# Head outputs turned by one transposing DMA per chunk, running sums accumulated in PSUM, and GpSimd's early work queued by the planner

## The chip, the cores and the metric

The kernel runs on one core of a Trainium2 chip. The metric is the device time of one execution in microseconds (us). The kernel before takes 731.63 us in the median of 3 runs (731.5 to 731.91).

## The reference

One input x of 2048 tokens by 512 features goes through two branches, and a gate mixes them per token.

```python
g = _sigmoid((x * gate_w).sum(-1, keepdims=True))
# A: 32 query heads of 16 dims, one shared K and V head
q = (x @ wq) as 32 heads;  k = x @ wk;  v = x @ wv
p = softmax(q k^T * 16 ** -0.5)        # 2048 x 2048 for each head
a = concat_heads(p @ v) @ wo           # 512 x 512
# B: gated MLP with a token-mixing matrix
z = gelu(x @ w_in)                     # 2048 x 1376
z1, z2 = z[..., :688], layernorm(z[..., 688:])
b = (z1 * (w_sp @ z2 + b_sp)) @ w_out  # w_sp is 2048 x 2048
return g * a + (1 - g) * b
```

All inputs and the output are bfloat16. Most of the work is the 32 x 2048 x 2048 exponentials of the softmax.

## The kernel before

**Units and blocks.** Attention is cut into 32 units: unit `u` is query chunk `c = u // 8` (512 queries) and four of the 32 heads. A unit has 64 blocks: 16 key tiles `kt` of 128 keys, times the four heads `g`. A block is one TensorE matmul of 32 rows (`s_mm`, tile `QA,KA`), one exponential of 128 x 512 scores, and one matmul with V that adds to the unit's output in a PSUM bank (`o_mm`). Two heads share 32 partitions of the queries `QA`. Even units read `KA[:, 0]`, where K fills the first 16 rows of each 32; odd units read `KA[:, 1]`, a copy shifted by 16 rows, which SyncE's queue (SP) makes by a DMA per chunk of 512 keys (`ld_K1`, L299). The input chunks arrive in the order `XO = (0, 3, 2, 1)`, so chunk 1, key tiles 4 to 7, is the last of the four.

**Two engines make the exponentials.** ScalarE (ACT) does most blocks, two or three at a time, by `Exp` from PSUM into the ring `P` (`exp_op`, L783). VectorE (DVE) does up to `NMAX` = 8 key tiles of a unit by a polynomial: `d_A` (L795) evacuates a block from PSUM into `UW[:, 0]`, `d_u` (L800) squares it, and `d_w` (L806) squares it again into `UW[:, 1]`; some of the `d_w` pieces go to GpSimd (POOL). Four blocks of one key tile are a batch. Both squares are multiplied with V on TensorE, and the constant and linear terms of the polynomial come from two small tables over V: `SVB` (sums of V, `g_SV`) and `KTV` (sums of K times V, `g_KTV`), each a running sum over the 8 key tiles. `KF` and `SF` are the fp32 sums, kept in the tail of tile `z1`, which the profile prints as `z`.

**After a unit.** DVE turns the unit's output out of PSUM (`t1_op`, L820). For two units together DVE takes a reciprocal, and POOL multiplies it by the gate (`rr`) and scales the output into `Tn` (`norm_ops`, L827). DVE turns `Tn` back by 32 x 32 blocks into `OT` (`t2_op`, L851). When the four pairs of a chunk are in `OT` and branch B's product `u` is there, `g_out` (L722) accumulates six matmul groups of branch B and four of `wo` with `OT` in one PSUM bank, and the result goes out. Chunk 3 is finished at the end by `g_part`, `g_fin` and `g_out` so that little is left after unit 31.

**The order is written by a planner.** `build_kernel` simulates PE, ACT and DVE with fixed costs (`C_MM`, `C_EV`, `A_OV`, ...) and emits each instruction when its turn comes, so each engine's program is a fixed list, run in order, with semaphore waits from the data dependencies. POOL's work is in two kinds: what is emitted on the spot, with its time only added up by `pool_t` (L404), and what waits in the queue `pl_q` until `pool_try` (L1604) finds that DVE will be reading PSUM for a while. SP has no clock in the planner. Each DMA of SP is put into SP's list when the planner reaches the call, and SP runs that list in order. A chained load (`sp_dma`, L276) waits on SP for the chained load before it to have landed. For the shifted copy of K the planner reckons a due time of its own:

```python
spc["free"] = max(spc["free"], t) + 650.0
T[("K1", c)] = spc["free"] + 2300.0
```

Before, the loads of `wo`, `wout` and the first quarter of `wT` (turned by DMA, four pieces) are issued by `g_K`'s `done` for the last chunk, right after that chunk's `ld_K1`. A second, general program for inputs on which the polynomial isn't safe follows behind a flag and is not executed here.

Of the kernel before, what the change touches and what calls it, by code (L numbers as in the profile page):

```python
# [19 lines left out]
NKT = 16  # L20
# [5 lines left out]
NQ = 3  # L26
# [32 lines left out]
PR = dict(HALF=100.0, IDR=10, IDN=4, WRES=16, D_HG=2500.0, D_FL=False, WIN=1000.0, WIH=560.0, BACK=32, PRESS=5, FLEX=3500.0, RMIN=32, WBL=0.5, W_MIN=0.9, HOLD=0.0, RLEND=0)  # L59
# [109 lines left out]
def build_kernel(nc, x_d, wq_d, wk_d, wv_d, wo_d, win_d, wsp_d, bsp_d, wout_d, gw_d, out_d):  # L169
    es = ExitStack()  # L170
    with es:
# [37 lines left out]
        OT = sb("OT", [128, 2, 4, 512], B16)  # L209
# [32 lines left out]
        wq_raw = UW[:, 1, ND - 1, :].bitcast(B16).rearrange("p (a n) -> p a n", a=4)  # L242
        z1 = z1f[:, 0:5 * S].rearrange("p (f t) -> p f t", t=S)
# [67 lines left out]
        def ld_wo(q):  # L311
            out = []
            for g in range(4):
                for jj in range(2):
                    out.append(q.dma_start(wo[32 * g + 16 * jj:32 * g + 16 * jj + 16, :, :],
                                           wo_d.rearrange("(jp r) n -> r jp n", r=128)[64 * jj + 16 * g:64 * jj + 16 * g + 16, :, :]))
            return out
# [38 lines left out]
        def mm(dst, lhsT, rhs, start, stop, r, w, tp=None, chan=None, tag=""):  # L356
            def fn(t):
                if tp is None:
                    return t.matmul(dst, lhsT, rhs, start=start, stop=stop)
                return t.matmul(dst, lhsT, rhs, start=start, stop=stop, tile_position=tp)  # L360
            return op("pe", fn, r=r, w=w, chan=chan, tag=tag)

# [60 lines left out]
        def g_K(c, lo=0, hi=512, b=BM):  # L423
# [8 lines left out]
            def done(t):  # L432
# [17 lines left out]
        def g_k2(c):  # L450
# [5 lines left out]
            def rdy():  # L456
                if not started:
                    if c and ("k2", c - 1) not in T:
                        return None
                    ksq()  # L460
                    started.append(pool_t(1150.0) + L_X)
                return started[0]
# [33 lines left out]
        def g_V(c, b=BM):  # L496
# [37 lines left out]
        def g_SV():  # L534
            n0 = NKT - NMAX

            def piece():
                fm(BM, 32 * NMAX, 0, ones[:], V1[:, n0:NKT, :].rearrange("p k w -> p (k w)"), True, True, ["ones", ("V", 2), ("V", 3)], "SV")
# [5 lines left out]
            def done(t):  # L544
                for i in range(NMAX - 2, -1, -1):
                    op("pool", lambda g, i=i: g.tensor_tensor(SF[:, i, :], SF[:, i, :], SF[:, i + 1, :], ALU.add), r=["SF"], w=["SF"], tag="SF")
                op("pool", lambda g: g.tensor_copy(SVB[:, 0:NMAX, :], SF), r=["SF"], w=["SVB"], tag="SVB")
                op("pool", lambda g: g.tensor_tensor(SVB[64:128, 0:NMAX, :], SF[64:128, :, :], SVB[64:128, 0:NMAX, :], ALU.subtract),
                   r=["SF", "SVB", ("z1", 5)], w=["SVB"], tag="SVB")
                T["SVB"] = pool_t(7 * 400.0 + 1200.0, t) + L_X  # L550
            return Group([(150.0, piece)], [(350.0, ev)], lambda: when(("V", 2), ("V", 3)), done, tag="SV")

        def g_KTV():
            n0 = NKT - NMAX

            def piece(k, e):
                def f():
                    for q in range(4):
                        o = 512 * BM + 64 * k + 32 * e
                        mm(ps[32 * q:32 * q + 32, o:o + 32], KN[:, k, e, :], V1[:, n0 + k, :], True, True,  # L560
# [3 lines left out]
            def ev():  # L564
                op("dve", lambda v: v.tensor_scalar(KF, bank(BM, 64 * NMAX).rearrange("p (k e w) -> p k e w", e=2, w=32), Q_C1, None, ALU.mult),
                   r=[bkey(BM), ("z1", 5)], w=["KF"], tag="KTVev")

            def done(t):
                for i in range(NMAX - 2, -1, -1):
# [5 lines left out]
            return Group([(26.0, piece(k, e)) for k in range(NMAX) for e in range(2)], [(C_EV, ev)], lambda: when(("V", 2), ("V", 3)), done, tag="KTV")  # L575

        def gate():
            op("act", lambda a: a.activation(E[:], gs[:], ACT.Exp), r=[("gs", k) for k in range(4)], w=["E"], tag="E")
            t = clk["now"] + 350.0
            for g in range(4):  # L580
                for k in range(4):
                    op("pool", lambda p, g=g, k=k: p.tensor_copy(RT[32 * g:32 * g + 32, :, :].rearrange("p c b -> p (c b)").rearrange("p (n k) -> p n k", k=4)[:, :, k],
                                                                E[32 * k:32 * k + 32, :]), r=["E"], w=["RT"], tag="RT")
            T["RT"] = pool_t(16 * 280.0, t) + L_X
# [18 lines left out]
        def gelu_ops():  # L603
            out = []
            for k in range(4):
# [32 lines left out]
                out.append((2400.0, f, []))  # L638
            for ft in range((NZ - ZD) // 4):
# [3 lines left out]
                out.append((1810.0, f, [("z1", ft, tc) for tc in range(4)]))  # L643
# [44 lines left out]
        def g_part(t2):  # L688
# [6 lines left out]
            def pw(jp):  # L695
                return lambda: fm(BM, 512, 0, OT[:, 1, jp, 128 * i:128 * i + 128], wo[:, jp, :], False, jp == 2, [("OT", 1, jp), "wo"], "wo")
# [4 lines left out]
            return Group([(C_MM, py(ft)) for ft in range(6)] + [(C_MM, pw(jp)) for jp in range(3)], [(C_EV + 50.0, ev)],  # L701
                         lambda: when(*([("u", ft, 3) for ft in range(6)] + [("OT", 3, jp) for jp in range(3)])), setT(("pt", i)), tag="part")

        def g_fin(t2, b, ready, eng):
# [3 lines left out]
            def piece():  # L708
                fm(b, 512, 0, OT[:, 1, 3, 128 * i:128 * i + 128], wo[:, 3, :], True, True, [okey, "wo"], "wo")
# [12 lines left out]
        def g_out(t2, b=BM, ready=None, on_act=False, eng="sp"):  # L722
# [67 lines left out]
        def o_mm(u, g, lhsT, rhs, r, last):  # L790
# [1125 lines left out]
```

## Time and profile before

| | |
|---|---|
| median of 3 runs | 731.63 us |
| the profiled execution, its own time | 731.97 us |
| its span in the trace | 730.0 us |
| busy: PE, DVE, ACT, POOL | 709.3, 711.0, 710.7, 471.9 us |
| ACT exponentials | 738 instructions, 1492 blocks |
| DVE batches | 139 |

The span is what the trace covers from the first instruction to the last; the execution's own time is 1.97 us longer. TensorE's busy time holds matmuls with zeros that the planner puts into idle stretches (tile `CT,zer`). In a timeline row the first number is the start in us and the second the time from the first instruction of the row to the end of its last; "x4" is the number of instructions that were merged. `[0.43 <-PE ps L360]` is idle time of the engine before the row, and what ended it.

### The profile page before, as it was taken

What the parts mean: (1) busy time and instruction counts of PE and PEld (TensorE: products, weight loads), DVE (VectorE), ACT (ScalarE), POOL (GpSimd) and SP (SyncE); (2) the same over time, 40 slices, a digit from 0 to 9 for tenths busy, and PEclk for the clock granted to TensorE, in tenths of its full rate; (3) what the DMA queues carried; (4) which work ended last, traced back from release to release, by engine and by line L of the source; (5) the groups of instructions that cost most, each with busy time, mean ns of one, the idle gap of its engine ahead of it and who ended that gap; (6) DMA issues with size and microseconds to landing.
All of it is one profiled execution on the core that took longest, in us unless ns stands there. A gap on an engine that the chain in (4) does not pass through costs nothing.

```text
span 730.0 us, 21704 instructions
## 1 busy us (share of the span) xinstructions
PE 709.3 (97%) x9004; PEld 207.4 (28%) x9004; DVE 711.0 (97%) x1028; ACT 710.7 (97%) x757; POOL 471.9 (65%) x439
## 2 busy tenths in 40 slices
PE   7999999999999999999999999999999999999996
PEld 3323333323322223222222232222222222222322
DVE  5999999999999999999999999999999999999996
ACT  5999999999999999999999999999999999999995
POOL 6743666670267777667576777777777766777662
PEclk9999999999999999999999999999999999999999
DMA  8342000000000002200000042000002400000000
GB/s 160 121 101 59 2 1 2 2 3 2 2 2 1 3 2 63 70 17 2 1 2 2 2 88 52 9 2 2 2 2 57 76 17 1 2 2 1 2 3 32
DMA packets 49119, 17.72 MB, mean 24 GB/s; under 512 B 44244, under 2 KB 48504, under 8 KB 49016
## 3 DMA queue, kind: packets, MB, share of 16 engines
q1 hardware_dynamic: 46760, 16.00, 9.4%
q8 instruction: 71, 1.16, 0.6%
q10 hardware_dynamic: 2256, 0.30, 0.3%
q14 instruction: 32, 0.26, 0.1%
HBM read 3.25 MB, written 2.10 MB: 7 GB/s over the span
## 4 chain that ended last, share of the span: by engine, by line
PE 59%; ACT 21%; DVE 11%; issue 7%; DMA 1%; ACTq 0%
PE ps L360 59%; ACT P L785 21%; DVE UW L797 4%; DVE bst L613 2%; DVE UW L810 2%; DVE UW L804 2%; DVE z L627 1%; DMA wvg<-in_gate_w_dram 1%; DVE T L822 0%; ACT z L607 0%; DVE mv L617 0%; DVE QA L486 0%; DVE Tn L845 0%; ACT L607 0%; DVE z L599 0%
## 5 line engine op out<-in xcount | busy, mean ns | idle before, releaser
L785 ACT ACTIVATE P<-ps 128x1024 bf16<-128x1024 f32 (+1 forms) x738 | 685.4, 1179 | 8.6 <-PE ps L360 8.3
L810 POOL TENSOR_TENSOR UW<-UW 128x512 f16<-128x512 f16 (+1 forms) x282 | 369.6, 1311 | 163.3 <-DVE UW L810 63.6
L797 DVE TENSOR_SCALAR UW<-ps 128x512 f16<-128x512 f32 (+1 forms) x414 | 347.7, 861 | 1.7 <-PE ps L360 1.1
L360 PE MATMUL ps<-QA,KA 32*128 32x512 bf16 x2048 | 311.7, 384 | 10.1 <-ACT P L785 5.3
L360 PE MATMUL ps<-P,V 128*32 128x512 bf16 x1492 | 207.2, 385 | 0.2 <-DVE KN L514 0.2
L804 DVE TENSOR_TENSOR UW<-UW 128x2048 f16<-128x2048 f16 (+1 forms) x166 | 174.4, 1052 | 1.1
L360 PEld LDWEIGHTS ps<-QA,KA 32*128 32x128 bf16 x2048 | 83.8, 91 | 310.8 <-ACT P L785 159.3
L360 PE MATMUL ps<-UW,VW 128*32 128x512 f16 x556 | 117.5, 384 | 0.2 <-DVE UW L810 0.2
L360 PE MATMUL ps<-wT,z 128*32 128x512 bf16 (+1 forms) x1536 | 115.9, 366 | 0.0
L810 DVE TENSOR_TENSOR UW<-UW 128x1024 f16<-128x1024 f16 (+4 forms) x173 | 112.3, 660 | 0.2
L360 PE MATMUL ps<-UW,V 128*32 128x512 f16 x556 | 83.9, 384 | 1.2 <-DVE T L822 0.7
L360 PEld LDWEIGHTS ps<-P,V 128*32 128x32 bf16 x1492 | 47.7, 94 | 52.4 <-issue 48.5
L490 POOL TENSOR_TENSOR QSQ<-QA 128x512 bf16<-128x512 bf16 x16 | 26.4, 1648 | 23.2 <-DVE UW L797 10.5
L360 PEld LDWEIGHTS ps<-wT,z 128*32 128x32 bf16 x1536 | 28.8, 94 | 43.2 <-issue 41.8
L360 PEld LDWEIGHTS ps<-UW,VW 128*32 128x32 bf16 x556 | 27.8, 94 | 15.9 <-issue 11.9
L360 PE MATMUL ps<-wout,z 128*32 128x512 bf16 x384 | 31.8, 384 | 0.0
L360 PE MATMUL ps<-win,xT 128*32 128x344 bf16 x512 | 31.0, 312 | 0.7 <-DVE QA L486 0.7
L845 POOL TENSOR_TENSOR Tn<-T,rc 128x512 bf16<-128x512 f32 x15 | 22.9, 1526 | 8.0 <-DVE UW L797 4.0
L360 PEld LDWEIGHTS ps<-UW,V 128*32 128x32 bf16 x556 | 19.6, 94 | 18.4 <-issue 11.7
L822 DVE STREAM_TRANSPOSE T<-ps 128x512 f32<-128x512 f32 (+1 forms) x33 | 22.7, 691 | 2.1 <-PE ps L360 1.9
L360 PE MATMUL ps<-CT,SVB 128*32 128x512 bf16 x128 | 22.9, 384 | 0.0
L360 PE MATMUL ps<-xT,win 128*32 128x512 bf16 (+1 forms) x384 | 22.5, 363 | 0.2 <-ACT P L785 0.2
(113 smaller groups left out, 373.2 us busy)
## 6 DMA issues: line engine op xcount, KB each, us to landing
out_dram<-outsb SPq DMA_DIRECT2D x15, 128.0 KB, 1.7
win<-in_B_w_in_dram SPq DMA_DIRECT2D x1, 1376.0 KB, 6.3
wout<-in_B_w_out_dram SPq DMA_DIRECT2D x1, 640.0 KB, 5.3
wo<-in_A_wo_dram SPq DMA_DIRECT2D x8, 64.0 KB, 2.3
KA<-KA SPq DMA_DIRECT2D x4, 112.0 KB, 2.3
UW<-in_A_wq_dram SPq DMA_DIRECT2D x1, 384.0 KB, 4.1
wT<-in_B_w_sp_dram SPq DMA_TRANSPOSE x16, 4.3
UW<-in_A_wq_dram ACTq DMA_DIRECT2D x1, 128.0 KB, 3.6
```

Source lines behind the costliest of these rows:

```text
L360: return t.matmul(dst, lhsT, rhs, start=start, stop=stop, tile_position=tp)
L490: dq(pl_q, 1050.0, lambda: op("pool", lambda v: v.tensor_tensor(QSQ[:, q % 2, :], QA[:, q % NQ, :], QA[:, q % NQ, :], ALU.mult), r=[("Q", ...
L613: dq(dve_q, 410.0, lambda st=st, h=h: op("dve", lambda v: v.bn_stats(bst[:, st, h, :], z2[:, FH * st + 344 * h:FH * st + 344 * h + 344]), ...
L627: op("pool" if st in ZP else "dve", lambda v: v.tensor_scalar(z2[:, FH * st:FH * st + FH], z2[:, FH * st:FH * st + FH], mv[:, st, 0:1], rs ...
L785: op("act", lambda a: a.activation(P[:, 512 * p0:512 * (p0 + n)], ps[:, 512 * b0:512 * (b0 + n)], ACT.Exp), r=[bkey(b0 + i_) for i_ in ran ...
L797: op("dve", lambda v: v.tensor_scalar(UW[:, 0, s, 512 * i:512 * (i + n)], bank(b, 512 * n), Q_A, Q_AS, ALU.mult, ALU.add), r=[bkey(b + j) ...
L804: op("dve", lambda v: v.tensor_tensor(src, src, src, ALU.mult), r=k, w=k, tag="dTT")
L810: op(eng, lambda v: v.tensor_tensor(UW[:, 1, s, 256 * a:256 * b], src, src, ALU.mult), r=[("U", s, h) for h in range(a // 2, (b + 1) // 2) ...
L822: return lambda: pgx.op("dve", lambda v: v.transpose(T1[:, jj, c0:c1], bank(BO, c1 - c0, c0)), r=[bkey(BO)], w=[("T1", jj, c0)], tag="T1")
L845: pgx.op(eng, lambda v: v.tensor_tensor(tnv[:, pr, j0:j1, b0:b1, :], t1v[:, j0:j1, b0:b1, 0:16], rc[:, j0:j1, b0:b1].unsqueeze(3).broadcas ...
```

## The change

1. **`OT` by DMA.** For all but the last pair of chunk 3, POOL writes the scaled outputs of a chunk into one 128 x 2048 tile `TB[c]` (the output buffer `outsb` for chunk 0, parts of `win` for the others), and one DMA on SP turns the whole chunk into `OT` (`t2_dma`). 15 DVE transposes go. The last pair of chunk 3 keeps the DVE transpose, into `OT3`, with a copy of its rows of `wo` in `wo3`; its place in the chunk's tile is zeroed, so chunk 3 has five `wo` groups instead of four.
2. **Running sums in PSUM.** `g_SV` and `g_KTV` let TensorE add up the running sums: matmul number k writes k + 1 columns groups by a broadcast V. The 14 adds on POOL go. `KF` becomes bfloat16, and the four copies of `KF` into `KTV` go from POOL to SP: four DMAs of 32 x 16 pieces of 32 elements.
3. **POOL's early work in `pl_q`.** `KSQ`, `VW`, `SVB` and the gate's table `RT` are queued.
4. **Loads.** The loads of `wo`, `wout` and `wT` move from the last `g_K` to `g_KTV`'s `done`, behind the `KTV` DMAs.
5. **Costs.** `A_OV`, `FLEX` and the gelu costs are raised a little. The planner then writes another order: 140 batches instead of 139, and on ACT 738 exponentials over 1488 blocks (720 of two blocks, 15 of three, 3 of one; before 718, 18 and 2).

```diff
-        KF = tmp[:, 0:64 * NMAX].rearrange("p (k e w) -> p k e w", e=2, w=32)
+        KF = tmp[:, 0:32 * NMAX].bitcast(B16).rearrange("p (k e w) -> p k e w", e=2, w=32)
...
         def ld_wo(q):
+            return [q.dma_start(wo[16 * r:16 * r + 16, :, :], wo_d[64 * r:64 * r + 64, :].rearrange("(g d) n -> d g n", g=4)) for r in range(8)]
...
                 elif hi == 512 and c == XO[3]:
                     ld_K1(c, t)
                     ld_bsp(0)
-                    sp_dma(ld_wo, w=["wo"], n=128)
-                    ld_rest()
...
-                    ksq()
-                    started.append(pool_t(1150.0) + L_X)
+                    started.append(None)
+                    dq(pl_q, 1150.0, ksq, clk["now"], setT(("ksq", c)))
...
             def done(t):
-                for i in range(NMAX - 2, -1, -1):
-                    op("pool", lambda g, i=i: g.tensor_tensor(KF[:, i, :, :], KF[:, i, :, :], KF[:, i + 1, :, :], ALU.add), r=["KF"], w=["KF"], tag="KF")
                 for q in range(4):
-                    op("pool", lambda g, q=q: g.tensor_copy(KTV[32 * q:32 * q + 32, :, :, q, :], KF[32 * q:32 * q + 32, :, :, :]),
-                       r=["KF", ("z1", 5)], w=["KTV"], tag="KTV")
-                T["KTV"] = pool_t(7 * 430.0 + 4 * 720.0, t) + L_X
+                    op("sp", lambda d, q=q: d.dma_start(KTV[32 * q:32 * q + 32, :, :, q, :], KF[32 * q:32 * q + 32, :, :, :]),
+                       r=["KF", ("z1", 5)], w=[("KTV", q)], dma=16, after=[o_ktv], tag="KTV")
+                T["KTV"] = t + 6000.0
+                sp_dma(ld_wo, w=["wo"], n=128)
+                ld_rest()
...
+        def t2_dma(c, t):
+            assert c < 2 or ("o", 4 * c - 5) in T, c
+            op("sp", lambda q: q.dma_start_transpose(OT[:, c % 2, :, :], TB[c]), r=TBK[c], w=[("OT", c % 2)], dma=16, tag="T2")
+            T[("OT", c)] = t + C_T2
...
-                dq(pl_q, C_TN, tn, (lambda: when(("rr", u))), setT(("TnE", u // 2)))
-                dq(t2_q, 625.0, t2_op(pg, c, jp, 0, 512, [("Tn", pr, 0, 0), ("Tn", pr, 1, 0)]), (lambda: when(("TnE", u // 2), *([("o", 4 * c - 5)] if c > 1 else []))), setT(("OT", c, jp)))
+                def tne(t):
+                    T[("TnE", u // 2)] = t
+                    if jp == (2 if c == 3 else 3):
+                        t2_dma(c, t)
+                dq(pl_q, C_TN, tn, (lambda: when(("rr", u))), tne)
```

**SP, first part of its list.** The rows below are SyncE's queue in the first 65 us: the shifted copies of K (`KA<-KA`), the load of `win`, and what follows. `f_d4`, `f_d12` and so on are semaphores, one for each DMA (or group of eight); `f_dve` is DVE's. Before:

```order
L300 DMA KA<-KA 112x512 [waits f_pool,f_dve]
L300 DMA KA<-KA 112x512
L300 DMA KA<-KA 112x512 [waits f_dve]
L306 DMA win<-in_B_w_in_dram 128x4x1376 [waits f_d4]
L300 DMA KA<-KA 112x512 [waits f_dve]
L309 DMA bspz<-in_B_b_sp_dram 1x512 [waits f_d12,f_pool]
L315 DMA wo<-in_A_wo_dram 16x4x512 [waits f_d14]
L315 DMA wo<-in_A_wo_dram 16x4x512 x7
L328 DMA wout<-in_B_w_out_dram 128x5x512 [waits f_d15]
L330 DMA wout<-in_B_w_out_dram 48x512 [waits f_d16,f_pool]
L330 DMA wout<-in_B_w_out_dram 48x512 [waits f_d17]
L322 DMA_TRANSPOSE wT<-in_B_w_sp_dram 128x16x128 [waits f_d18]
```

Of the changed kernel, from the row behind `win` on:

```order
L591 DMA KTV<-z 32x16x32 [waits f_dve]
L591 DMA KTV<-z 32x16x32 x3
L318 DMA wo<-in_A_wo_dram 16x4x512 [waits f_d12]
L318 DMA wo<-in_A_wo_dram 16x4x512 x7
L345 DMA wout<-in_B_w_out_dram 128x5x512 [waits f_d17]
L347 DMA wout<-in_B_w_out_dram 48x512 [waits f_d18,f_pool]
L347 DMA wout<-in_B_w_out_dram 48x512 [waits f_d19]
L339 DMA_TRANSPOSE wT<-in_B_w_sp_dram 128x16x128 [waits f_d20]
L339 DMA_TRANSPOSE wT<-in_B_w_sp_dram 128x16x128 [waits f_d21]
L339 DMA_TRANSPOSE wT<-in_B_w_sp_dram 128x16x128 [waits f_d22]
L339 DMA_TRANSPOSE wT<-in_B_w_sp_dram 128x16x128 [waits f_d23]
L306 DMA KA<-KA 112x512 [waits f_dve]
```

The fourth copy of K, that of chunk 1, stood ahead of the loads of `wo`, `wout` and `wT`; it now stands behind all of them, and its semaphore is `f_d25` (before: `f_d13`).

**PE, where that copy is first read.** The rows are TensorE's list around the first matmul of unit 1 on key tiles 4 to 7 (`QA,KA` with a wait for the copy); `f_pes`, `f_pep` and `f_act` are semaphores of PE and ACT. Before:

```order
L360 MATMUL ps<-UW,VW 32x512 [waits f_dve]
L360 MATMUL ps<-P,V 32x512
L360 MATMUL ps<-UW,VW 32x512
L360 MATMUL ps<-QA,KA 128x512 [waits f_act,f_d13]
L360 MATMUL ps<-QA,KA 128x512
L360 MATMUL ps<-xT,wqd 32x512 [waits f_dve]
L360 MATMUL ps<-xT,wqd 32x512 x7
```

Of the changed kernel:

```order
L377 MATMUL ps<-xT,wqd 32x512 x4
L377 MATMUL ps<-P,V 32x512 x4
L377 MATMUL ps<-QA,KA 128x512 [waits f_act]
L377 MATMUL ps<-QA,KA 128x512 [waits f_d25]
L377 MATMUL ps<-P,V 32x512 x4
L377 MATMUL ps<-CT,zer 32x512 x4
L377 MATMUL ps<-UW,V 32x512 [waits f_dve]
```

The matmul stands at nearly the same place of the program: behind 97 matmuls of scores instead of 96, in ACT's 36th instead of its 37th exponential.

**DVE, where `KTV`'s sums leave PSUM.** The rows are DVE's list around the evacuations of `SF` and `KF` (both `z<-ps`). Before:

```order
L541 TENSOR_SCALAR z<-ps 128x256 [waits f_pe]
L797 TENSOR_SCALAR UW<-ps 128x512 [waits f_pes] x2
L804 TENSOR_TENSOR UW<-UW 128x2048 [waits f_dve]
L565 TENSOR_SCALAR z<-ps 128x512 [waits f_pe]
L797 TENSOR_SCALAR UW<-ps 128x1024 [waits f_pes]
```

Of the changed kernel:

```order
L565 TENSOR_SCALAR z<-ps 128x256 [waits f_pe]
L816 TENSOR_SCALAR UW<-ps 128x512 [waits f_pes]
L823 TENSOR_TENSOR UW<-UW 128x2048 [waits f_dve]
L816 TENSOR_SCALAR UW<-ps 128x1024 [waits f_pes]
L586 TENSOR_SCALAR z<-ps 128x512 [waits f_pe]
```

The evacuation of `KF` now follows one evacuation of 128 x 1024 that it was ahead of before.

More of the change, by code (lines that the diff above doesn't have):

```diff
@@ L256, in build_kernel @@
         op("dve", lambda v: v.memset(wk_rep[:], 0.0), w=["wk_rep"])
+        o_ktv = op("dve", lambda v: v.memset(KTV[:], 0.0), w=[("KTV", q) for q in range(4)])
         op("dve", lambda v: v.memset(V1[:], 0.0), w=[("V", c) for c in range(4)])
@@ L361, in mm, with wo_g @@
             return op("pe", fn, r=r, w=w, chan=chan, tag=tag)
+        def wo_g(b, c, i, g, start, stop, r):
+            for q in range(4):
+                mm(ps[32 * q:32 * q + 32, 512 * b:512 * b + 512], OT[:, c % 2, 4 * i + q, 32 * g:32 * g + 32], wo[:, g, :], start, stop, r, [bkey(b)],
+                   tp=(0, 32 * q), tag="wo")
         def fm(b, n, off, lhsT, rhs, start, stop, r, tag):
@@ L642, in f @@
                     T[("gelu", ft)] = clk["now"] + 2000.0
-                out.append((1810.0, f, [("z1", ft, tc) for tc in range(4)]))
+                out.append((1905.0, f, [("z1", ft, tc) for tc in range(4)]))
             return out
@@ L844, in d @@
             def d():
-                pgx.op(eng, lambda v: v.tensor_tensor(tnv[:, pr, j0:j1, b0:b1, :], t1v[:, j0:j1, b0:b1, 0:16],
+                dst = TB[c].rearrange("p (b z j w) -> p z j b w", z=4, j=2, w=16)[:, jp, :, :, :] if big else tnv[:, pr, j0:j1, b0:b1, :]
+                aft = list(pgx.ops["dve"][-2:-1]) if eng == "pool" else []
+                if big and c and jp == 0:
+                    assert dz["i"] >= NZ and dz["cur"] is None
+                    aft += pg.readers["win"][-1:]
@@ L1183, in f @@
                         def f(last, g=g, n=n, u=pu):
-                            o_mm(u, g, KTV[:, NMAX - n, u % 2, g, :], QA[:, (u // 2) % NQ, :], ["KTV", ("Q", (u // 2) % NQ)], last)
+                            o_mm(u, g, KTV[:, NMAX - n, u % 2, g, :], QA[:, (u // 2) % NQ, :], [("KTV", q) for q in range(4)] + [("Q", (u // 2) % NQ)], last)
                             if g == 3:
@@ L1357, in dz_act @@
                     T[("gelu", ft)] = t + L_X
-            return now + act_period(n)
+            return now + act_period(n) + 90.0
         def pe_work(now):
```

125 lines of the change are left out of this document (73 added, 52 removed).

## The prediction

> **What bounds the kernel now.** I read the page first, then ACT's groups by shape, the windows behind 45 us, ACT's waits, and last the rows of the two queues that the change reorders. The page:
>
> ```profile
> span 730.0 us, 21704 instructions
> PE 709.3 (97%) x9004; PEld 207.4 (28%) x9004; DVE 711.0 (97%) x1028; ACT 710.7 (97%) x757; POOL 471.9 (65%) x439
> ```
>
> Three engines look equally full, so the page alone doesn't say who leads. The windows (PE, PEld, DVE, ACT, POOL busy, then clock and DMA; the sum is over all five from 45 to 720 us) and ACT's waits do:
>
> ```profile
> 60.00:160.00 100.00, 97.89 (x1257) 30.82 (x1257) 99.24 (x138) 100.00 (x108) 62.57 (x51) 1.00 0.03 7
> ...
> 240.00:700.00 460.00, 457.64 (x5537) 125.55 (x5529) 457.14 (x626) 460.00 (x501) 326.26 (x272) 1.00 0.08 19
> ...
> sum 675.00, PE 665.50 PEld 191.08 DVE 670.17 ACT 672.94 POOL 440.00; mean PE 133.10 PEld 38.22 DVE 134.03 ACT 134.59 POOL 88.00
> ...
> ACT P L785 <- PE ps L360: 8.3, 10, 5.3
> ```
>
> From 60 to 160 and from 240 to 700 us ACT is busy for every microsecond; in the 675 us from 45 to 720 it idles 2.1. PE and DVE idle more there and are led by it: the end is ACT's number of exponentials, and whatever stops ACT. Of its 8.3 us of waits on PE, 5.3 are the start. ACT's work by shape:
>
> ```profile
> L785 ACT ACTIVATE P<-ps 128x1024 bf16<-128x1024 f32 x718 | 664.0, 1171 | 2.9 <-PE ps L360 2.7
> L785 ACT ACTIVATE P<-ps 128x1536 bf16<-128x1536 f32 x18 | 28.3, 1570 | 5.3 <-PE ps L360 5.3
> L785 ACT ACTIVATE P<-ps 128x512 bf16<-128x512 f32 x2 | 1.2, 594 | 0.3 <-PE ps L360 0.3
> ```
>
> An instruction overlaps the next, so its price is busy time over count: 664.0 / 718 = 0.925 us for two blocks, 28.3 / 18 = 1.57 for three, 0.6 for one.
>
> **The path that decides: the fourth copy of K.** Rows of the SP queue from 24 us on, the landing times (last number, us), and PE and ACT at the matmul that needs the copy of chunk 1:
>
> ```profile
> 28.22 0.51 SPq L300 DMA_DIRECT2D KA<-KA  x1
> ...
> 30.31 3.62 SPq L315 DMA_DIRECT2D wo<-in_A_wo_dram  x8
> 35.73 0.39 SPq L328 DMA_DIRECT2D wout<-in_B_w_out_dram  x1
> 41.05 2.07 SPq L330 DMA_DIRECT2D wout<-in_B_w_out_dram  x2
> 44.46 16.53 SPq L322 DMA_TRANSPOSE wT<-in_B_w_sp_dram  x4
> ...
> SPq L322 <- DMA wT<-in_B_w_sp_dram: 8.8, 3, 4.0
> ...
> KA<-KA SPq DMA_DIRECT2D x4, 112.0 KB, 2.3
> wT<-in_B_w_sp_dram SPq DMA_TRANSPOSE x16, 4.3
> ...
> 45.06 0.39 PE L360 MATMUL ps<-QA,KA 32*128 32x512 bf16 x2
> ...
> 45.38 0.61 PE L360 MATMUL ps<-xT,wqd 128*32 128x512 bf16 x8
> 45.52 1.02 ACT L785 ACTIVATE P<-ps 128x1024 bf16<-128x1024 f32 x1 [0.43 <-PE ps L360]
> ```
>
> In the trace the copy is issued at 28.22 and lands 2.3 later, 14 us before the matmul at 45.06 reads it. The loads behind it take SP from 30.31 to 60.99 (44.46 + 16.53), because each waits for the one before to land (8.8 us of waits among the `wT` pieces). In the changed kernel the copy stands behind these loads, and the matmul that needs it has kept its place. The planner's due time for the copy doesn't see SP's list. So:
>
> 1. `KF`'s evacuation. It frees the `KTV` DMAs, and with them the loads.
>
> ```profile
> 23.40 0.68 DVE L565 TENSOR_SCALAR z<-ps 128x512 f32<-128x512 f32 x1
> 24.00 1.21 DVE L797 TENSOR_SCALAR UW<-ps 128x1024 f16<-128x1024 f32 x1
> ```
>
> It ended at 24.1; now the 1.21 us evacuation stands ahead of it: 25.3. Bounds 24.1 (nothing moves) and 26.2 (`KTV`'s wider matmuls on PE push it too).
>
> 2. Four `KTV` DMAs. The trace has no DMA like them; a copy of K took 0.51 to issue, and `win` and `wk_sb`, both 512 pieces, show these rows:
>
> ```profile
> 18.24 0.59 SPq L306 DMA_DIRECT2D win<-in_B_w_in_dram  x1
> wk_sb<-in_A_wk_dram ACTq DMA_DIRECT2D x1, 16.0 KB, 2.1
> ...
> 36.21 0.38 PE L360 MATMUL ps<-QA,KTV 128*32 128x512 bf16 x2
> ```
>
> I take 0.55 each, 2.2 (bounds 1.8 and 2.4). The table itself lands about 2.1 later, near 30: PE's first matmul with it in the trace is at 36.2, so this wait costs nothing.
>
> 3. From the first `wo` load to the end of the last `wT` issue: 30.7 as traced. Its first `wT` piece held SP for 6.0 and the others for 4.3:
>
> ```profile
> 44.46 7.86 SPq L322 DMA_TRANSPOSE wT<-in_B_w_sp_dram  x2
> 50.47 6.14 SPq L322 DMA_TRANSPOSE wT<-in_B_w_sp_dram  x2
> 54.72 6.27 SPq L322 DMA_TRANSPOSE wT<-in_B_w_sp_dram  x2
> ```
>
> (44.46 to 50.47 to 54.72.) Whether that delay comes again is open; I take 30.0, bounds 29.0 and 32. Then 2.4 for the copy to land (2.3, or behind the last turned piece, which itself lands 4.3 after its start).
>
> Sum: 25.3 + 2.2 + 30.0 + 2.4 = **59.9 us**, between 57.1 and 63. PE runs its list in order, so everything behind that matmul waits: V products, evacuations on DVE, and ACT, which has at most two steps of scores in PSUM. The matmul starts 14.9 us later than at 45.06, and ACT's next exponential with it. Nothing gives this back later: ACT was busy without a gap.
>
> **PE after the stop.** PE's clock over the first matmuls, and the same shape later:
>
> ```profile
> 1.44 4.21 PE L359 MATMUL ps<-CT 128*128 128x512 bf16 x11 [1.44 <-DVE CT L255]
> L359 PE MATMUL ps<-CT x11: 379/634/634, 1.4 to 5.3; 128*128 128x512 bf16 x11
> L360 PE MATMUL ps<-CT,zer x176: 377/379/392, 20.7 to 723.1; 128*32 128x512 bf16 x176
> ```
>
> (min/median/max ns.) The first eleven matmuls ran at 634 ns, later ones at 379; at the later pace (0.22 for each further 512 columns, by 0.61 − 0.39 of the x8 row above) they would have taken 2.6 us instead of 4.21. Whether PE is slow again after about 15 idle us, no row shows: the bounds are 0 and 1.6 + 0.25 for the waiting matmul itself. I take 1.5 in all, since the start is the only row behind a long idle time.
>
> [...]
>
> **The rest of the change.**
> - *Exponentials.* 2 × 0.925 − 3 × 1.57 + 1 × 0.6 = −2.3 us; one block (0.5) of it lies before the stop and is swallowed there: −1.8.
> - *15 DVE transposes of 0.70 go*; one batch, smaller evacuations and smaller squares come:
>
> ```profile
> L853 DVE STREAM_TRANSPOSE OT<-Tn 128x512 bf16<-128x512 bf16 x15 | 10.5, 702 | 0.0
> L797 DVE TENSOR_SCALAR UW<-ps 128x512 f16<-128x512 f32 x272 | 175.6, 678 | 0.9 <-PE ps L360 0.5
> L797 DVE TENSOR_SCALAR UW<-ps 128x1024 f16<-128x1024 f32 x142 | 172.2, 1212 | 0.8 <-PE ps L360 0.6
> ```
>
> Evacuations go to 286 and 137: 14 × 0.65 − 5 × 1.21 = +3.0. DVE ends some 5 us lighter, but ACT's idle time behind 45 us is 2.1 in all, so this can bring 0 to 2.1; I take 1.0.
> - *POOL's early work.* While POOL multiplied, DVE's squares stretched:
>
> ```profile
> 41.11 1.04 POOL L490 TENSOR_TENSOR QSQ<-QA 128x512 bf16<-128x512 bf16 x1
> 41.32 1.91 DVE L804 TENSOR_TENSOR UW<-UW 128x2048 f16<-128x2048 f16 x1
> L804 DVE TENSOR_TENSOR UW<-UW 128x2048 f16<-128x2048 f16 x112 | 137.4, 1227 | 0.9
> ```
>
> 1.91 against 1.23, and ACT's short waits before 45 us come from such places. Whatever is saved there is time in front of the stop and is swallowed: 0. The adds that left POOL cost 0 for the same reason.
> - *`OT`'s DMAs.* The turned tile has `wT`'s shape, 4.3 us, on a queue that is otherwise idle. The tightest use is the last:
>
> ```profile
> 684.85 1.43 POOL L845 TENSOR_TENSOR Tn<-T,rc 128x512 bf16<-128x512 f32 x1 [0.45 <-DVE UW L797]
> 691.82 0.61 PE L360 MATMUL ps<-wo,OT 128*32 128x512 bf16 x8
> ```
>
> `Tn` ends at 684.85 + 1.43 = 686.3, and the DMA at 686.3 + 4.3 = 690.6, before 691.8: 0.
> - *Chunk 3's fifth `wo` group*: 16 more matmuls, 0.9 us of PE, in front of PE's filler with zeros; 0 (bound 0.9).
>
> **Sum.** 730.0 + 14.9 + 1.5 − 1.8 − 1.0 = 743.6 of span. The profiled execution's own time is 2.0 above its span (731.97) and the median of the runs 0.3 below that: 743.6 + 2.0 − 0.3 = 745.3 us.
>
> **Rivals.**
> 1. *The copy is in time, and the change is faster.* If the copy landed before 45 us, as it would if SP didn't hold it behind the chained loads, ACT would never stop: −2.3, −1.0 and up to 2 of the 3.0 us of short waits, 731.6 − 5.3 = 726.3 us. Against it: SP's waits for landings stand in the trace. It decides only if the chain took under 15 us instead of 30. Chance 0.05.
> 2. *The turned tile is late.* If a transposing DMA out of SBUF takes 10 us rather than the 4.3 of `wT` (no row shows one with this source), PE waits in front of `part` near the end, 686.3 + 10 − 691.8 = 4.5 us more, on top of the stop: 749.8 us. For it: PE runs in order and its list has no slack there; against it: same shape, idle queue. Chance 0.08.
> 3. *DVE's relief counts in full.* If ACT's pace (460.00 / 501 = 0.918 an instruction) were held down by DVE's lateness, its 5 us net would show instead of 1.0: 745.3 − 4 = 741.3 us. Against it: ACT has no gaps in the windows. Chance 0.06.
>
> **How the numbers follow.** The forecast keeps 0.81, and its bounds added one way give 739.9 to 750.6. All at one end is unlikely; 741.5 to 749.5 leaves about 2 in 10 outside, with rivals 1 and 3 mostly below and half of rival 2 above. 0.2% (1.5 us) is about what a measurement of this kernel can tell from no change. Only rival 1 is faster: 0.05; within 0.2% would need the stop to be just paid back: 0.01; slower 0.94.
>
> **What would show it.** In the changed profile: SP's fourth `KA<-KA` issued near 57.5 us instead of 28.2; one wait of PE on that DMA of 14 to 18 us near 42 to 60; ACT and DVE empty in the same slices of the page; some matmuls of 634 ns behind it; from there on ACT gapless at 0.92 an instruction; no DVE rows `OT<-Tn` but two small ones. The forecast is wrong if the copy's issue stands before 45 us, or if PE's wait there is under 10 us.

## The result, and the profile after

The changed kernel takes 748.87 us in the median of 4 runs (747.47 to 751.62), against 731.57 (731.01 to 731.91) for the kernel before on the same chip: the ratio is 1.024, with a 95% interval of 1.021 to 1.027. The profiled execution took 748.98 us. Its page, with the busy totals and three rows of the 40 slices (18.7 us each):

```profile
span 747.2 us, 21846 instructions
PE 714.1 (96%) x9048; PEld 210.7 (28%) x9048; DVE 704.9 (94%) x1035; ACT 708.7 (95%) x757; POOL 471.3 (63%) x440
...
PE   8927999999999999999999999999999999999996
ACT  5936999999999999999999999999999999999995
PEclk9977999999999999999999999999999999999999
```

The busy totals hardly moved: ACT did 2.0 us less than before, DVE 6.1 less. The 17 us are the dent in slices 3 and 4, where PE and ACT stand still in the same stretch. SP's rows ahead of the dent, and PE's first row behind it:

```profile
25.52 3.41 SPq L591 DMA_DIRECT2D KTV<-z  x4
28.98 3.90 SPq L318 DMA_DIRECT2D wo<-in_A_wo_dram  x8
34.82 0.39 SPq L345 DMA_DIRECT2D wout<-in_B_w_out_dram  x1
39.03 2.08 SPq L347 DMA_DIRECT2D wout<-in_B_w_out_dram  x2
42.50 14.98 SPq L339 DMA_TRANSPOSE wT<-in_B_w_sp_dram  x4
57.53 0.59 SPq L306 DMA_DIRECT2D KA<-KA  x1
...
60.30 0.60 PE L377 MATMUL ps<-QA,KA 32*128 32x512 bf16 x1 [18.10 <-DMA KA<-KA]
```

The copy of K chunk 1 is issued at 57.53 us; before it was issued at 28.22. PE stood for 18.10 us in front of the matmul that reads it. The windows (PE, PEld, DVE, ACT, POOL busy, granted clock, DMA share, GB/s) show the stop and what follows it:

```profile
45.00:60.00 15.00, 0.00 (x0) 0.00 (x0) 0.00 (x0) 0.00 (x0) 0.09 (x1) 0.53 0.60 136
60.00:65.00 5.00, 4.71 (x42) 1.34 (x46) 0.00 (x0) 2.59 (x3) 0.00 (x0) 0.50 0.01 3
65.00:70.00 5.00, 5.00 (x67) 1.54 (x59) 4.31 (x7) 4.04 (x4) 1.04 (x1) 0.87 0.00 0
...
240.00:700.00 460.00, 459.80 (x5507) 127.59 (x5503) 456.81 (x627) 459.97 (x502) 330.54 (x285) 1.00 0.10 23
```

ACT's timeline behind the stop:

```profile
60.94 1.02 ACT L804 ACTIVATE P<-ps 128x1024 bf16<-128x1024 f32 x1 [17.84 <-PE ps L377]
62.94 1.45 ACT L804 ACTIVATE P<-ps 128x1536 bf16<-128x1536 f32 x1 [0.98 <-PE ps L377]
64.89 1.02 ACT L804 ACTIVATE P<-ps 128x1024 bf16<-128x1024 f32 x1 [0.50 <-PE ps L377]
66.87 10.12 ACT L804 ACTIVATE P<-ps 128x1024 bf16<-128x1024 f32 x10 [0.96 <-PE ps L377]
```

From 60 to 65 us the granted clock is 0.50, and ACT waits 0.98 + 0.50 + 0.96 = 2.4 us more. (In e1 below, where the stop is taken away, ACT makes the same exponentials without a gap.) From 240 to 700 us it is gapless again, with 502 exponentials in place of 501: nothing is given back.

### The profile page after: what moved, and what is told of

The parts are those of the page before. It is cut to its first block, busy times and chain, and to the rows that moved or that the text cites. A ratio compares the mean times of both kernels' runs of the same rounds, so it can differ in the third digit from the quotient of the medians.

```text
span 747.2 us, 21846 instructions
## 1 busy us (share of the span) xinstructions
PE 714.1 (96%) x9048; PEld 210.7 (28%) x9048; DVE 704.9 (94%) x1035; ACT 708.7 (95%) x757; POOL 471.3 (63%) x440
## 4 chain that ended last, share of the span: by engine, by line
PE 69%; DVE 11%; ACT 10%; DMA 4%; issue 4%; SPq 1%; ACTq 0%; DVEq 0%
PE ps L377 69%; ACT P L804 9%; DVE UW L816 4%; DVE bst L635 2%; DMA wT<-in_B_w_sp_dram 2%; DVE UW L823 2%; DVE UW L829 1%; DMA wout<-in_B_w_out_dram 1%; DVE z L649 1%; DMA xT<-in_A_x_dram 1%; SPq L591 0%; SPq L318 0%; DMA KA<-KA 0%; ACT z L629 0%; DMA wo<-in_A_wo_dram 0%
## 5 line engine op out<-in xcount | busy, mean ns | idle before, releaser
L804 ACT ACTIVATE P<-ps 128x1024 bf16<-128x1024 f32 (+1 forms) x738 | 683.5, 1185 | 27.0 <-PE ps L377 26.7
L829 POOL TENSOR_TENSOR UW<-UW 128x512 f16<-128x512 f16 (+1 forms) x300 | 375.4, 1251 | 156.1 <-DVE UW L829 63.8
L377 PE MATMUL ps<-P,V 128*32 128x512 bf16 x1488 | 204.7, 386 | 0.4 <-issue 0.3
L823 DVE TENSOR_TENSOR UW<-UW 128x2048 f16<-128x2048 f16 (+1 forms) x176 | 177.9, 1011 | 1.3
L377 PEld LDWEIGHTS ps<-QA,KA 32*128 32x128 bf16 x2048 | 86.1, 91 | 325.6 <-ACT P L804 151.7
L377 PE MATMUL ps<-UW,VW 128*32 128x512 f16 x560 | 119.5, 384 | 0.0
L829 DVE TENSOR_TENSOR UW<-UW 128x1024 f16<-128x1024 f16 (+4 forms) x176 | 109.0, 634 | 1.9 <-POOL UW L829 1.9
L621 DVE CAST z<-ps 128x344 bf16<-128x344 f32 x32 | 16.2, 506 | 21.2 <-PE ps L377 21.1
L377 PEld LDWEIGHTS ps<-UW,VW 128*32 128x32 bf16 x560 | 27.9, 94 | 17.3 <-issue 14.5
L377 PEld LDWEIGHTS ps<-UW,V 128*32 128x32 bf16 x560 | 19.9, 95 | 19.6 <-issue 14.9
L472 POOL TENSOR_TENSOR KSQ<-KA 128x512 bf16<-128x512 bf16 x4 | 5.6, 1408 | 31.3 <-PE ps L377 31.2
L377 PE MATMUL ps<-QA,KTV 128*32 128x512 bf16 x128 | 23.3, 383 | 0.0
```

What stands on the lines that cost most here:

```text
L472: op("pool", lambda g: g.tensor_tensor(KSQ[:], KA[:, 0, 512 * c:512 * c + 512], KA[:, 0, 512 * c:512 * c + 512], ALU.mult), r=[("K0", c), ...
L621: ev = lambda: op("dve", lambda v: v.tensor_copy(z2[:, FH * st + 344 * h:FH * st + 344 * h + 344], bank(BM, 344)), r=[bkey(BM)], w=[("z2", ...
L804: op("act", lambda a: a.activation(P[:, 512 * p0:512 * (p0 + n)], ps[:, 512 * b0:512 * (b0 + n)], ACT.Exp), r=[bkey(b0 + i_) for i_ in ran ...
L823: op("dve", lambda v: v.tensor_tensor(src, src, src, ALU.mult), r=k, w=k, tag="dTT")
L829: op(eng, lambda v: v.tensor_tensor(UW[:, 1, s, 256 * a:256 * b], src, src, ALU.mult), r=[("U", s, h) for h in range(a // 2, (b + 1) // 2) ...
```

## The experiments

**Is the stop the whole loss?** In e1 the loads alone go back to where they were:

```diff
 # g_K, done
                     ld_K1(c, t)
                     ld_bsp(0)
+                    sp_dma(ld_wo, w=["wo"], n=128)
+                    ld_rest()
 # g_KTV, done
                 T["KTV"] = t + 6000.0
-                sp_dma(ld_wo, w=["wo"], n=128)
-                ld_rest()
```

> The changed kernel with one thing undone: the chained loads of wo, wout and wT are issued again behind the fourth copy of K (and the bspz row), so SP's list is KTV x4, KA<-KA, bspz, wo, wout, wT. Everything else of the change stays; no other engine's list changes. Theory (the copy queued behind chained loads is the whole loss): the fourth KA<-KA is issued near 29 us, PE does not wait for it, and the time is that of the changed kernel less the stop of 18.1 us and less 2 to 3 us of slow start behind it: 728 us (726 to 729.5). Rival 1 (the KTV or OT transfers themselves, or their traffic, slow the kernel): most of the loss stays, 740 us or more. Rival 2 (the rest of the change brings nothing): 731 to 732 us, the time of before.

Measured: 728.18 us (727.86 to 728.55), ratio to before 0.994 (0.9925 to 0.9959). SP's rows, and the window in which ACT passes the place of the stop:

```profile
25.95 3.90 SPq L593 DMA_DIRECT2D KTV<-z  x4
29.90 0.63 SPq L306 DMA_DIRECT2D KA<-KA  x1
...
32.26 4.70 SPq L318 DMA_DIRECT2D wo<-in_A_wo_dram  x8
...
45.00:60.00 15.00, 14.27 (x195) 4.83 (x192) 14.62 (x19) 15.00 (x16) 3.22 (x3) 1.00 0.40 82
```

ACT's waits on PE (total, times, longest), in the changed kernel and then in e1:

```profile
ACT P L804 <- PE ps L377: 26.7, 9, 17.8
```

```profile
ACT P L804 <- PE ps L377: 6.8, 5, 4.9
```

The copy goes out at 29.90, ACT's waits on PE fall from 26.7 us to 6.8 (4.9 of them the start), and 20.7 of the changed kernel's 748.9 us go (21.4 if each is set against the kernel before in its own set of runs: 17.3 above, 4.1 below). Rival 1 of this expectation is out, since the four `KTV` DMAs and `OT`'s DMAs are all still there. So is its rival 2: what is left of the change is 3 to 4 us faster than before.

The other way round, e2 makes that one move in the kernel before:

```diff
 # before.py, g_K, done
-                    sp_dma(ld_wo, w=["wo"], n=128)
-                    ld_rest()
 # g_KTV, done
+                sp_dma(ld_wo, w=["wo"], n=128)
+                ld_rest()
```

> The kernel before with this one part of the change alone: the loads of wo, wout and wT are issued where the KTV group is done, ahead of the fourth copy of K; sums on POOL, OT by DVE and all the rest as before. Theory: win lands near 25.8 us, the chain then takes 30.7 as traced before, the copy is issued near 56.5 and lands near 58.9, PE's matmul that started at 45.06 waits until then: stop 13.8, slow start 2 to 3, 748 us (745 to 750). Rival (the loss comes from other parts of the change, and the move of the loads is harmless): 731 to 733 us.

Measured: 748.73 us (745.54 to 749.6), ratio 1.021 (1.018 to 1.024). The copy and PE's wait stand in the trace as expected; the windows behind the stop follow them:

```profile
56.74 0.59 SPq L300 DMA_DIRECT2D KA<-KA  x1
...
59.50 0.60 PE L360 MATMUL ps<-QA,KA 32*128 32x512 bf16 x2 [13.65 <-DMA KA<-KA]
...
60.00:65.00 5.00, 5.00 (x38) 0.84 (x36) 2.35 (x3) 3.78 (x4) 0.45 (x1) 0.50 0.02 3
65.00:70.00 5.00, 5.00 (x46) 1.16 (x42) 2.83 (x5) 3.39 (x4) 2.01 (x2) 0.50 0.00 0
```

Part 4 of the change alone makes the loss; taken away, the loss is gone. The slow start is longer here than in the changed kernel: half clock lasts until 71.45 us, 12 us behind the stop, and ACT's waits in it sum to 0.55 + 0.43 + 0.49 + 0.43 + 0.78 = 2.7 us, against 0.45 + 0.17 = 0.6 at the same place in the kernel before.

**How the loss grows with the stop.** In e3 and e6 the copy stands behind one piece of `wT`, and behind none:

```diff
-        def ld_wT(tc):
-            for k in range(4):
+        def ld_wT(tc, ks=range(4)):
+            for k in ks:
...
-            ld_wT(0)
+            ld_wT(0, range(1))              # e6: range(0)
...
                     ld_K1(c, t)
+                    ld_wT(0, range(1, 4))   # e6: range(0, 4)
```

> The changed kernel with the fourth copy of K placed behind the first piece of wT instead of behind all four. Theory: the copy is issued near 44.5 us (first wT piece issued at 42.50 for 1.97) and lands near 47.0; PE waits from 42.2 on for about 4.8 us instead of 18.1. If the loss is the stop in proportion, the time is that of e1_loads_back plus 4.8: near 733 us; if a stop of this length already brings the granted clock down to half, 2 to 3 us more, near 735. Rival (a fixed loss that does not hang on the length of the stop, or a loss elsewhere): 740 us or more. [...]

> The changed kernel with the fourth copy of K placed behind wo and wout, ahead of all four pieces of wT. The copy is issued near 41.7 us and lands near 44.0, where PE waits for it from 42.2 on: a stop of about 1.8 us. If a stop this short leaves the granted clock alone, the time is that of e1_loads_back plus 2.0: 730.2 us (729.5 to 731), and no matmul of over 0.5 us stands behind it. If any stop at all brings the slow start, the loss is that of e3_short_stop (8.3 us, landing at 47.9) less 3.9: 4.4 us, 732.6. [...]

Measured: e3 736.52 us (736.05 to 736.79), e6 732.15 (729.16 to 733.91). That is 8.3 and 4.0 us above e1. ACT's rows of e3, then of e6:

```profile
48.89 1.02 ACT L805 ACTIVATE P<-ps 128x1024 bf16<-128x1024 f32 x1 [6.00 <-PE ps L377]
50.89 1.45 ACT L805 ACTIVATE P<-ps 128x1536 bf16<-128x1536 f32 x1 [0.98 <-PE ps L377]
52.84 1.02 ACT L805 ACTIVATE P<-ps 128x1024 bf16<-128x1024 f32 x1 [0.50 <-PE ps L377]
54.70 14.22 ACT L805 ACTIVATE P<-ps 128x1024 bf16<-128x1024 f32 x14 [0.84 <-PE ps L377]
```

```profile
44.32 1.02 ACT L805 ACTIVATE P<-ps 128x1024 bf16<-128x1024 f32 x1 [1.14 <-PE ps L377]
46.01 1.45 ACT L805 ACTIVATE P<-ps 128x1536 bf16<-128x1536 f32 x1 [0.67 <-PE ps L377]
47.95 1.02 ACT L805 ACTIVATE P<-ps 128x1024 bf16<-128x1024 f32 x1 [0.50 <-PE ps L377]
49.26 14.22 ACT L805 ACTIVATE P<-ps 128x1024 bf16<-128x1024 f32 x14 [0.29 <-PE ps L377]
```

In e3 the waits, 6.00 + 0.98 + 0.50 + 0.84 = 8.3 us, agree with the loss; 736.52 us is 1.5 above the longer of the two times expected. The slow start costs as much behind a stop of 6 us (2.3) as behind one of 18 (2.4): here it did not grow with the stop. In e6 the shorter of the two times, 730.2, had none, and there it is again, 0.67 + 0.50 + 0.29 = 1.5 us behind 1.1 us of stop; the longer, 732.6, was the nearer. (These rows give 2.6 of e6's 4.0 us. In its trace 1.0 us more than in e1 arises behind the last exponential; why is not shown, and its runs spread over 4.8 us.) PE's rows of e6 show when the clock falls:

```profile
43.90 0.38 PE L377 MATMUL ps<-QA,KA 32*128 32x512 bf16 x1 [1.62 <-DMA KA<-KA]
44.21 0.40 PE L377 MATMUL ps<-P,V 128*32 128x512 bf16 x4
44.44 0.50 PE L377 MATMUL ps<-CT,zer 128*32 128x512 bf16 x4
44.71 0.65 PE L377 MATMUL ps<-UW,V 128*32 128x512 f16 x4
...
47.24 0.61 PE L377 MATMUL ps<-QA,KA 32*128 32x512 bf16 x3
...
48.77 0.39 PE L377 MATMUL ps<-QA,KA 32*128 32x512 bf16 x3
```

PE idled only 1.62 us, and the first matmuls behind that still took 0.38; those of 0.5 us and more begin half a microsecond into the work and last until about 47.9. The granted clock of this trace is 0.50 from 44.58 to 47.99.

**Is the slow start the clock, or the refilling of the pipeline?** In e4, e5 and e12, 72, 304 and 400 matmuls with zeros stand straight in front of the waiting matmul:

```diff
 # s_mm
+            if u == 1 and kt == 4 and not kept:
+                kept.append(1)
+                for i in range(72):         # e5: 304, e12: 400
+                    q = i % 4
+                    mm(ps[32 * q:32 * q + 32, 512 * dst_bank:512 * dst_bank + 512], zer[:, 32 * q:32 * q + 32], CT[:], True, True, ...)
             mm(bank(dst_bank), KA[...], QA[...], True, True, ...)
```

> The changed kernel with 72 matmuls with zeros (tile CT,zer) placed on PE straight in front of the matmul that waits for the copy, into the bank that this matmul overwrites: 72 x 0.22 = 15.8 us of the 18.1 us in which PE had nothing to do. The stop itself stays. Theory 1 (the slow start behind the stop is the granted clock, which falls while PE idles): the matmuls behind the stop take 0.38 and not 0.61 us, ACT's idle time between 60 and 70 us falls from 3.1 to under 1 us, and the time falls by 2 to 3 us to 746.4 (745.5 to 747). Theory 2 (the slow start is the refilling of the pipeline behind an empty stretch): the time stays within 0.7 us of the changed kernel's 748.9.

Measured: 749.77 us (749.48 to 750.41). This run missed its aim. Four such matmuls run beside each other (in this trace four of `P,V`, of the same shape, took 0.39 us together, and one of `QA,KA` 0.39), and all 72 were over in 4.07 us, 0.057 each, so PE idled 17.1 us all the same. The slow start came too, with 0.98 + 0.30 + 0.20 = 1.5 us of waits.

> As e4_pe_kept_busy, but 304 matmuls with zeros instead of 72. In e4 the 72 matmuls were over 4 us after the first, since four of them run beside each other on the four column groups: 0.054 us each in place of the 0.22 that was reckoned, so PE idled 18 us all the same. 304 x 0.054 = 16.4 us. The copy's landing varies by 2 to 3 us with the loads, so the test is the rows: PE's matmuls behind the stop, and ACT's three waits there, 0.98 + 0.50 + 0.96 = 2.4 us in the changed kernel. Theory 1 (the granted clock falls while PE idles): the matmuls take 0.38 us from the first on, the three waits sum to under 0.8 us, and the time is 746.6 us (745 to 748) if the copy lands as in the changed kernel. Theory 2 (a pipeline that refills): matmuls may be fast, the three waits still sum to about 2 us, 748.5 us.

Measured: 751.28 us (749.78 to 753.53). The zeros ended at 58.9, the copy landed later than in the changed kernel, PE idled 3.64 us, and 28 matmuls of over 0.45 us followed (PE's rows from 62.54 to 64.90 took 0.49 to 0.64); the waits sum to 0.98 + 0.20 + 0.21 = 1.4. Still not clean.

> As e5_pe_kept_busy_304 with 400 matmuls with zeros. In e5 they ended at 58.6 us, and PE still idled 3.6 us before the copy landed; its matmuls behind that took 0.61 to 0.63 us for 3.7 us. 400 x 0.054 = 21.6 us last beyond the landing (near 61 us), so that PE goes from the zeros straight to the waiting matmul. Theory 1 (the granted clock falls while PE idles): no matmul behind the zeros takes over 0.5 us, and ACT's waits behind the stop, 2.4 us in the changed kernel and 1.4 in e5, sum to under 0.8. Theory 2 (the refilling of the pipeline): the matmuls are fast and the waits still sum to 1.4 or more. The time itself hangs on where the loads land and on up to 2 us of surplus zeros: 747 to 751 us by both.

Measured, in one execution: 751.51 us. PE's rows, then ACT's:

```profile
65.99 0.38 PE L377 MATMUL ps<-QA,KA 32*128 32x512 bf16 x1 [2.40 <-DMA KA<-KA]
66.31 0.40 PE L377 MATMUL ps<-P,V 128*32 128x512 bf16 x4
...
66.42 14.93 ACT L811 ACTIVATE P<-ps 128x1024 bf16<-128x1024 f32 x14 [23.61 <-PE ps L377]
```

Here no matmul behind the stop is slow, and ACT, after a stop of 23.61 us, has no wait at all behind it. The pipeline was as empty as in the changed kernel, so theory 2 falls: the 2.4 us are the granted clock. ACT's waits go with the time at half clock behind the stop, not with the length of the stop: 2.4 and 2.3 us for about 6 us of it (changed kernel, e3), 1.4 to 1.5 for 3.4 to 4.0 (e4, e5, e6), nothing for none (e12). As a cure the zeros are useless, since the stop remains; the loads landed later in these three kernels (the matmul that waits for the copy started at 62.54 to 65.99 us, 60.30 in the changed kernel; why is not shown), which is why they are no faster.

**What the rest of the change is worth.** e7 is the kernel before with parts 2, 3 and 5, e8 with part 5, e9 with part 1 (the diff's hunks of these parts, nothing else); e10 is e1 once more beside them.

> The same kernel as e1_loads_back, beside the three others on the same chip: 728.2 us (727.5 to 728.9) by both theories. It is the measure for e7, e8 and e9, and the version that beats both kernels if its interval stays below 1.

> The kernel before with parts 2, 3 and 5 of the change (sums in PSUM, GpSimd's early work queued, costs), without part 1 (OT stays on DVE) and part 4 (the loads stay behind the fourth copy of K). ACT then has 726 exponentials of two blocks, 14 of three and 2 of one, against 720, 15 and 3. At ACT's periods in the traces (0.918, 1.339, 0.65 us) that is 3.5 us more than e1_loads_back. Theory 1 (what is left of the gain is the count of exponentials, and ACT's short waits up to 60 us): 728.2 + 3.5 = 731.7 us (730.7 to 732.7), with ACT's waits up to 60 us as short as in e1. Theory 2 (the 15 transposes on DVE cost more than their effect on the count, up to 5 us): 734 us or more. Theory 3 (the count doesn't matter): 728 to 729.

> The kernel before with part 5 of the change alone, the planner's costs. ACT has 734 exponentials of two blocks, 7 of three and 3 of one, against 718, 18 and 2: at the periods 0.918, 1.339 and 0.65 us, 0.6 us more. Theory: 732.1 + 0.6 = 732.7 us (731.7 to 733.7). Rival (the order written with these costs is by itself the better one, and the operations that change are not): 728 to 730 us.

> Part 1 of the change alone: OT by DMA; the sums of V and KV on POOL, POOL's early work, the costs and the place of the loads are as before. ACT has 714 exponentials of two blocks, 19 of three and 3 of one: 0.15 us less than e1_loads_back by the periods. ACT idles 2.6 us more between 20 and 60 us in the trace of before than in that of e1. Theory 1 (those short waits come from POOL's early work and stay here): 728.2 + 2.6 - 0.2 = 730.6 us (729.8 to 731.4). Rival (they have another cause, or are paid back later): 728 us.

| | median, us | ratio to before, 95% |
|---|---|---|
| before, beside them | 731.98 | |
| e10 (all but part 4) | 728.69 | 0.9955 (0.9942 to 0.9968) |
| e7 (parts 2, 3, 5) | 731.32 | 0.9989 (0.998 to 0.9998) |
| e8 (part 5) | 733.09 | 1.0016 (1.0007 to 1.0025) |
| e9 (part 1) | 740.89 | 1.0135 (1.0116 to 1.0153) |

e7 is 2.6 us above e10, where theory 1 had 3.5, theory 2 at least 5.8 and theory 3 next to nothing. So the transposes that leave DVE seem to pay through the number of exponentials that ACT needs; that is argued from the size, not shown by a run of its own. The costs alone (e8) lose 1.1 us. ACT's short waits up to 60 us stay in e8 and go in e7, as the same window shows for before, e7, e8 and e1, in this order:

```profile
20.00:60.00 40.00, 37.08 (x543) 11.51 (x536) 39.97 (x53) 37.48 (x42) 23.90 (x43) 1.00 0.40 110
```

```profile
20.00:60.00 40.00, 38.70 (x601) 13.26 (x589) 38.99 (x57) 39.59 (x43) 16.62 (x26) 1.00 0.42 113
```

```profile
20.00:60.00 40.00, 37.10 (x538) 11.52 (x535) 39.86 (x54) 37.53 (x43) 23.84 (x43) 1.00 0.40 110
```

```profile
20.00:60.00 40.00, 38.79 (x606) 13.71 (x602) 39.30 (x58) 39.56 (x43) 17.44 (x27) 1.00 0.41 105
```

ACT's busy time in these 40 us rises from 37.53 us in e8 to 39.59 in e7: 2.1 us that parts 2 and 3 bring. (Which of the two it is was not tried.)

e9 lies 10 and 13 us above its two expectations (the 2.6 us in the first of them are 2.1 by the windows above). Its SP rows near 560 us, and PE's:

```profile
554.34 16.81 SPq L339 DMA_TRANSPOSE wT<-in_B_w_sp_dram  x4
573.31 0.26 SPq L315 DMA_DIRECT2D bspz<-in_B_b_sp_dram  x1
573.67 1.72 SPq L877 DMA_TRANSPOSE OT<-win  x1
...
577.97 1.04 PE L377 MATMUL ps<-wo,OT 128*32 128x512 bf16 x8 [8.74 <-DMA OT<-win]
```

It is the same mechanism a second time. In this order the planner called for the last quarter of `wT` a few us ahead of chunk 2's `OT` DMA, and that DMA stood behind the chained pieces although POOL had finished its tile at 558.5. The changed kernel escapes it only because its order has the two calls the other way round. e11 moves that one DMA behind the first piece:

```diff
-                    ld_wT(tc + 1)
+                    ld_wT(tc + 1, range(1 if tc == 2 else 4))
...
             if c == 2:
+                ld_wT(3, range(1, 4))
```

> The kernel of e9_ot_dma_alone with one thing moved on SP: chunk 2's OT DMA stands behind the first of the four pieces of wT's last quarter instead of behind all four. In e9 the tile it turns was complete at 558.5 us, the DMA was issued at 573.67, and PE waited 8.7 us for it. Theory (the loss of e9 is that place in SP's list, and nothing else of OT by DMA): PE does not wait for OT, ACT's 10.5 us of idle time between 560 and 580 us fall to about 0.3, and the time is 740.9 - 10.2 = 730.7 us (730 to 732.5, since the later pieces of wT land some 2 us later). Rival (a transposing DMA out of SBUF is slow when it meets other loads): PE still waits for OT, 735 us or more.

Measured: 730.4 us, ratio 0.998 (0.9971 to 0.9989). The DMA is issued as soon as its tile is there, and PE has no wait for `OT`:

```profile
554.74 1.84 SPq L339 DMA_TRANSPOSE wT<-in_B_w_sp_dram  x1
558.96 2.01 SPq L879 DMA_TRANSPOSE OT<-win  x1
561.02 11.49 SPq L339 DMA_TRANSPOSE wT<-in_B_w_sp_dram  x3
```

So part 1 at a good place in SP's list is worth 1.5 us, parts 2, 3 and 5 are worth 0.7, and all of them together 3.3 (e10), more than the sum of 2.2. Why was not tried, but the planner writes a new order for each combination, and the counts of exponentials do not add up either: at ACT's periods of 0.918, 1.339 and 0.65 us they are worth an estimated 1.7 us in e11 (714 of two blocks, 19 of three, 3 of one), −2.0 in e7 (726, 14, 2) and 1.5 in e10 (720, 15, 3), so 1.8 us more together than alone. e1 is the version that beats both kernels: 3.3 to 4.1 us under before in two sets of runs, 20 us under the changed kernel.

## Why the prediction was right

It foretold the mechanism, its place and most of its size: 745.3 us, with 748.9 measured, inside 741.5 to 749.5 but near its upper end; a loss of 13.7 us forecast and 17.3 measured. The span came out at 747.2 instead of 743.6. By its steps:

1. **`KF`'s evacuation** ended near 25.5 us (the first `KTV` DMA is issued at 25.52), forecast 25.3.
2. **The four `KTV` issues** took 3.41 us, not 2.2, and beyond the bound of 2.4: one of the four took 1.31 us, the others 0.63 to 0.70.
3. **The chain of loads** took 28.98 to 57.48 = 28.5 us, not 30.0, and beyond its lower bound: the long delay behind the first `wT` piece did not come again (the four pieces took 14.98 us from the first row to the end of the last, 16.53 before). That the two misses nearly cancel is luck. The matmul started at 60.30 against 59.9 (0.3 us of the miss in the sum, which gave 14.9 us for 45.06 to 60.30). The lower bound of that sum, 57.1, adds up to 57.2 from its own terms.
4. **The slow start** was the mis-sized term: 2.4 us against 1.5, and over its bound of 1.85. I had reckoned it from PE's time alone at the start; ACT, which pays for it, waits through three steps (0.98 + 0.50 + 0.96). That PE is slow again behind about 15 idle us no row of before showed; the 1.5 was an estimate from the 634 ns matmuls of the start. In the changed kernel's trace 0.50 is granted from 45.81 to 66.29 us.
5. **The rest of the change** behind the stop, forecast at 1.8 + 1.0 = 2.8 us, was worth about 1.1: e1's span is 3.2 us under that of before (726.8 against 730.0), and 2.1 of that lies ahead of 60 us, where the stop swallows it, as step "POOL's early work" said. The price of 1.57 us for an exponential of three blocks was too high: in e1's and before's traces one starts 1.34 us after the other, which makes the count worth 1.5 and not 2.3.
6. **`OT`'s DMAs** cost nothing in the changed kernel, as forecast; they landed 3.6 to 4.7 us behind their issue.

These make 0.3 + 0.9 + 1.7 = 2.9 of the 3.6 us; ACT's wait of 0.5 us between 75 and 160 us, which before did not have, is most of the remainder.

Of the rivals, the first (the copy in time) is what e1 builds: 728.2 to 728.7 us, against its 726.3. The second (the turned tile late) did not happen here, but its argument that the list has no slack did: in e9 the wait came, from the queue and not from a slow transfer. The third (DVE's relief in full) fell: ACT's pace from 240 to 700 us is the same.

## What to carry to other kernels

Here a DMA that was put into a queue's list waited for every wait ahead of it in that list (the copy of K was issued at 57.53 us instead of 28.22, e9's `OT` DMA at 573.67 with its tile ready at 558.5), so whoever moves a chain of loads must look for the small, urgent transfer that ends up behind it; a planner that gives transfers due times without a clock for the queue cannot see it. Such a stop on an in-order engine was paid nearly in full by the engine that leads (18.10 us on PE, 17.84 on ACT in the changed kernel), and behind it came a slow start of TensorE that cost 1.4 to 2.4 us whether the stop was 1 us or 18, and nothing where matmuls with zeros had filled the stop but for its last 2.40 us (e12). When a change has several parts and loses, take the parts back one at a time: here two misplaced calls cost 20 us and hid a gain of 3 to 4.

## What the runs showed of the hardware

- **Half clock around the stops lasted 3.41 to 23.89 us.** The granted clock stood at 0.50 for 3.41 us in e5 and e6 (62.69 to 66.10, 44.58 to 47.99), 10.24 in e3 and e9 (43.76 to 54.00, 571.09 to 581.33), 17.07 in e4, 20.48 in the changed kernel (45.81 to 66.29) and 23.89 in e2 (until 71.45).
- **The longer of two short idle times was not the one with half clock.** In e6 PE idled 1.62 us, and the clock was at 0.50 from 44.58 us on, 0.68 behind the start of the next matmul (43.90). In e12 PE idled 2.40 us, and the rows behind that took 0.38 and 0.40 us, where those of e6 at 0.50 took 0.61; why is not shown. Nor did a busy PE bring full clock back at once: in e2 PE was busy for all of the 10 us from 60 to 70, with 0.50 granted throughout, and its slow start was twice as long as the changed kernel's (12 us at half clock behind the stop against 6); the reason is open.
- **The four `KTV` issues did not take the same time in every trace.** In the changed kernel they took 3.41 us, one of them 1.31 and the shortest 0.63, in e1 3.90, in e6 2.72:

```profile
25.61 2.72 SPq L592 DMA_DIRECT2D KTV<-z  x4
```
